# Lead and first block as one list of steps, kept by five queues

## The chip, the cores and the metric

One core of a Trainium2 chip runs the program. A core has a matrix engine (PE), a vector engine (DVE), an activation engine (ACT), a general one (POOL) and SP, which here only issues transfers (the load queue). Every engine works its own queue in order and waits on semaphores for the others. The metric is the device time of one execution in microseconds (us); less is better.

## What is computed

Three layers in a row, all in float32; the first is attention with a complex decay:

```python
mag = np.sqrt(a_re * a_re + a_im * a_im)
scale = np.minimum(mag, 0.999) / (mag + 1e-06)      # a_re, a_im times scale
for t in range(S):                                   # B, H, S, D = 4, 8, 768, 48
    S_re, S_im = ar*S_re - ai*S_im + outer(k, v), ar*S_im + ai*S_re
    y[:, :, t] = einsum(q, S_re)
x = y as 3072 rows of 384
h = x @ w_in;  g = h * tanh(softplus(h));  x = g @ w_out      # d_ff 2048
out = ((x @ w_a) * (x @ w_b)) @ w_out2                         # d_ff 1536
```

## The kernel before, in words

The 768 steps are cut into 6 chunks of 128 for each of 4 batches, so there are 24 chunks c = 0 to 23; block j is the four chunks 4j to 4j+3, 512 rows of x. In a chunk the decay is squared (`decay_1`, step `sq`), added (`add`), taken through Ln and Exp on ACT (`ln`, `ex`), made into an angle (`tan`, `at`) and a size (`ell`); running sums over the chunk are matmuls (`pl`, `pt`); q and k are scaled (`sc`) and rotated (`rq`, `rk`), transposed on PE and copied out by ACT (`tq`, `tk`, `cq`, `ck`), multiplied (`s`), masked on DVE (`cp`), multiplied with v (`py`), and the result is split into a high and a low half for PE (`xh` on ACT, `xl` on DVE). `outer` and `state` (`ou`, `sd`, `st`) bring the state forward.

The second layer is 16 units f for each block. A unit is nine matmuls (`moe1_h`, called h below), a minimum on DVE (mn), four activations (ma, mb), a product on DVE (pr) and the matmuls of `moe1_x2` (x). A block of the third layer has 12 units of 18 and 12 matmuls. The weights of the second layer come as 64-bit numbers: a transfer of 768 KB each (w), then three DVE operations (`decode`: da, dc, db), a rounded copy on ACT (hi, so) and a subtraction on POOL (lo, sl). There are two buffers `wraw` for raw weights, so a third transfer waits until the first is decoded. In block 0 the weights of `w_out` are used as decoded; they are split for block 1 and later.

Before the change only the lead (chunks 0 to 3, three decodes) follows a list written out by hand, kept on DVE, ACT, PE and POOL by `in_order`; the load queue isn't in it. In the lead `load_a` loads the decay of a chunk in two transfers of 192 KB, real and imaginary part; both go by SP, except that the imaginary part of chunk 0 is issued on ACT's queue. `load_a(0)` also loads ACT's Ln/Exp table. From block 0 on the program states the steps unit by unit: chunk steps come at slots (`plan`, `run_to`), weights by `pipeline`, one call of `do_w` a unit. A scheduler of the framework then orders each queue by that sequence and a model of costs, and may take steps out of turn. `behind` keeps the first units after the lead.

ps_h has two buffers, so the h of unit n+2 waits until pr of unit n has read its sum.

Of the kernel before, what the change touches and what calls it, by code (L numbers as in the profile page):

```python
# [21 lines left out]
def kernel(  # L22
# [118 lines left out]

    def load_weights(nm, j, src, pool, place, late=False):

        a, b = src.shape[1:]
        if src.dtype == F32:
            raw = pool.tile([P, a, b], F32, tag="wraw", name="wraw", bufs=2)
            nc.sync.dma_start(out=raw, in_=src)
        else:  # L150
            b //= 2
            raw = pool.tile([P, a, b, 2], U32, tag="wraw", name="wraw", bufs=2)
            nc.sync.dma_start(out=raw.rearrange("p a b t -> p a (b t)"), in_=src)
        f = [raw]

        def decode(first=True, rest=True):
            if late and first:
                f[0] = wps[0].tile([P, a, b], F32, tag="f", name=f"w{nm}{j}", bufs=NF // 2 + 1)
                whole[nm, j] = f[0], split
                if src.dtype == F32:  # L160
                    nc.vector.tensor_copy(f[0], raw)
                    return
            if src.dtype != F32:
                if not late and first:
                    f[0] = pool.tile([P, a, b], F32, tag="wf32", name="wf32")
                fu, low, high = f[0].bitcast(U32), raw[..., 0], raw[..., 1]
                if first:
                    nc.vector.tensor_scalar(fu, high, 3, 0x3FFFFFFF, ALU.logical_shift_left, ALU.bitwise_and)
                    nc.vector.scalar_tensor_tensor(fu, high, 0xC0000000, fu, ALU.bitwise_and, ALU.bitwise_or)  # L169
                if rest:  # L170
                    nc.vector.scalar_tensor_tensor(fu, low, 29, fu, ALU.logical_shift_right, ALU.bitwise_or)

        def split():
            hi = place(f"w{nm}h{j}", [P, a, b])
            if late:
                lo = wps[0].tile([P, a, b], F32R, tag="f", name=f"w{nm}l{j}", bufs=NF // 2 + 1)
            else:
                lo = place(f"w{nm}l{j}", [P, a, b])
            weights[nm, j] = [hi, lo]
            act(out=hi, in_=f[0], func=AF.Copy)  # L180
            nc.gpsimd.tensor_tensor(lo, f[0], hi.bitcast(F32), ALU.subtract)

        return [decode, lambda: None] if late else [decode, split]
# [77 lines left out]
    def in_rows(c, nm):  # L261
# [4 lines left out]
        if nm == "qh":  # L266
            nc.gpsimd.memset(own[:, :, D:], 0.0)
# [77 lines left out]
    def decay_exp(c):  # L345
# [100 lines left out]

    def values(c):
# [4 lines left out]
        if not j:  # L452
# [28 lines left out]
    def store_y2(c):  # L481
        j, b = chunk(c)
        if not j:
            return
        py, yh, yl = st.pop(("y", c))
        nc.vector.tensor_tensor(yl, py, yh.bitcast(F32), ALU.subtract)
        for y, d in zip((yh, yl), yt_d[j]):
            for par in range(2):
# [3 lines left out]
                )  # L492

# [29 lines left out]
    def read_x(c):  # L523
# [4 lines left out]
        if not j:  # L528
# [125 lines left out]

    def load_w2(early):


        for j in range(NF2 // 2):
            def place(name, shape, j=j):
                if j == EARLY:  # L660
                    return wps[0].tile(shape, F32R, tag="f", name=name, bufs=NF // 2 + 1)
# [129 lines left out]
    def pipeline(steps, ahead, loaded=(), decoded=()):  # L791

        loaded, decoded = list(loaded), list(decoded)
# [13 lines left out]
    weights1 = None  # L807

    def do_w():
        next(weights1, None)  # L810

# [20 lines left out]
    def lead_in():  # L832

        for c in range(B):
            load_a(c)
        decode, split = steps1[0]()
        for c in range(B):
            load_qk(c)
        for c in range(B):
            load_v(c)  # L840
        decode_2, split_2 = steps1[1]()
        run_to(slot[0] + 1)
        w_in_1 = steps1[2]()

        def size(c):
            decay_4(c)
            split_ell(c)
# [312 lines left out]
```

## Time and profile before

| | us |
|---|---|
| three timed runs | 1089.99, 1091.11, 1091.15 |
| median | 1091.11 |
| the profiled execution, its own time | 1091.89 |
| its span, first to last instruction | 1090.2 |
| PE busy | 1049.1 (96%) |
| DVE busy | 655.7 (60%) |
| ACT busy | 610.5 (56%) |
| POOL busy | 231.4 (21%) |

The profile is of one execution. All times inside it count from the first instruction. A matmul's end is modelled and consecutive matmuls overlap, so the distance from start to start tells what one costs; the same holds in a smaller measure for DVE and ACT.

### The profile page before, as it was taken

To read this page: it belongs to the slowest core of one execution; us is meant where nothing else is said; L and a number is where in the kernel's file an instruction comes from. 1 tells how busy PE (TensorE), PEld (TensorE's weight loads), DVE (VectorE), ACT (ScalarE), POOL (GpSimd) and SP (SyncE) were. 2 spreads that over 40 slices of the span, in tenths; PEclk is the share of its full clock that TensorE was granted. 3 is DMA by queue.
4 is the path that set the end of the run, shared out by engine and by line. 5 is a ranking of instruction groups with operands and counts; after the bars stand their busy time and mean duration, and the time that the engine had idled before them with its cause. 6 is when DMAs were issued, how large, how long until landed. Compare 5 with 4: busy or idle time off the path is not lost.

```text
span 1090.2 us, 15919 instructions
## 1 busy us (share of the span) xinstructions
PE 1049.1 (96%) x6060; PEld 874.8 (80%) x6060; DVE 655.7 (60%) x998; ACT 610.5 (56%) x968; POOL 231.4 (21%) x265
## 2 busy tenths in 40 slices
PE   4979999999999999999999999999999999999997
PEld 1956666788888888888877778888888888888886
DVE  6898976787777777777589998532322322422222
ACT  7868887898788887788767842221221222212211
POOL 2122333444334334333331123100000000000000
PEclk9999999999999999999999999999999999999999
DMA  9656652354444343343155366110100100100000
GB/s 199 140 155 170 166 152 66 67 96 86 112 81 81 67 95 79 83 102 79 31 164 182 126 217 211 44 58 1 30 29 1 58 1 1 44 1 1 29 1 32
DMA packets 203549, 90.92 MB, mean 83 GB/s; under 512 B 144781, under 2 KB 187850, under 8 KB 203466
## 3 DMA queue, kind: packets, MB, share of 16 engines
q1 hardware_dynamic: 202410, 89.62, 32.9%
q8 instruction: 50, 0.82, 0.3%
q10 hardware_dynamic: 1056, 0.21, 0.1%
q14 instruction: 33, 0.27, 0.1%
HBM read 72.44 MB, written 17.36 MB: 82 GB/s over the span
## 4 chain that ended last, share of the span: by engine, by line
PE 72%; DVE 12%; ACT 6%; issue 4%; DMA 3%; POOL 2%; SPq 1%; ACTq 0%; DVEq 0%; POOLq 0%
PE x2ps L639 12%; PE ops L719 12%; PE hps L596 12%; PE psa L694 11%; PE psb L694 11%; PE psc L435 3%; PE py L465 3%; ACT m L59 3%; PE pkT L412 2%; PE pqT L412 2%; DVE wf L169 1%; ACT L54 1%; DVE m L602 1%; PE pt L331 1%; PE pu L504 1%
## 5 line engine op out<-in xcount | busy, mean ns | idle before, releaser
L705 DVE TENSOR_TENSOR a_sb<-a_sb,psb 128x512 f32<-128x512 f32 x72 | 49.4, 686 | 224.6 <-PE psb L694 224.6
L59 ACT ACTIVATE m<-m 128x512 f32<-128x512 f32 x192 | 119.4, 632 | 62.5 <-DVE m L602 57.7
L59 ACT ACTIVATE a_sb<-psa 128x512 f32<-128x512 f32 x72 | 42.9, 596 | 162.8 <-PE psa L694 160.7
L59 ACT ACTIVATE ph<-a_sb 128x512 fp32r<-128x512 f32 x72 | 45.4, 631 | 156.7 <-DVE a_sb L705 156.7
L596 PE MATMUL hps<-xh,winh 128*128 128x512 f32 x288 | 118.9, 414 | 7.8 <-DVE gh L613 6.4
L623 POOL TENSOR_TENSOR gl<-m,gh 128x512 fp32r<-128x512 f32 x64 | 83.2, 1300 | 151.7 <-DVE gh L622 128.4
L596 PE MATMUL hps<-xl,winh 128*128 128x512 f32 x288 | 114.0, 396 | 0.0
L596 PE MATMUL hps<-xh,winl 128*128 128x512 f32 x288 | 113.9, 396 | 0.0
L719 PE MATMUL ops<-woh,ph 128*128 128x384 f32 x288 | 97.1, 337 | 0.0
L719 PE MATMUL ops<-woh,pl 128*128 128x384 f32 x288 | 97.1, 337 | 0.0
L719 PE MATMUL ops<-wol,ph 128*128 128x384 f32 x288 | 96.7, 336 | 0.0
L639 PE MATMUL x2ps<-gl,wouth 128*128 128x512 f32 x240 | 94.3, 393 | 2.2 <-DVE gl L623 1.2
L639 PE MATMUL x2ps<-gh,wouth 128*128 128x512 f32 x240 | 94.1, 405 | 1.8 <-ACT gh L59 1.5
L639 PE MATMUL x2ps<-gh,woutl 128*128 128x512 f32 x240 | 94.0, 392 | 0.0
L616 DVE SCALAR_TENSOR_TENSOR m<-m,hps 128x512 f32<-128x512 f32 x80 | 54.7, 684 | 62.3 <-ACT m L59 61.5
L694 PE MATMUL psa<-xh,wal 128*128 128x512 f32 x216 | 85.2, 394 | 0.0
L694 PE MATMUL psa<-xl,wah 128*128 128x512 f32 x216 | 85.1, 394 | 0.0
L694 PE MATMUL psa<-xh,wah 128*128 128x512 f32 x216 | 84.4, 391 | 0.6 <-DVE a_sb L705 0.6
L694 PE MATMUL psb<-xh,wbh 128*128 128x512 f32 x216 | 84.2, 390 | 0.0
L694 PE MATMUL psb<-xh,wbl 128*128 128x512 f32 x216 | 84.2, 390 | 0.0
L694 PE MATMUL psb<-xl,wbh 128*128 128x512 f32 x216 | 84.2, 390 | 0.0
L707 DVE TENSOR_TENSOR pl<-a_sb,ph 128x512 fp32r<-128x512 f32 x72 | 52.0, 722 | 39.0 <-ACT ph L59 39.0
(167 smaller groups left out, 2335.8 us busy)
## 6 DMA issues: line engine op xcount, KB each, us to landing
wraw<-in_moe_w_out_dram SPq DMA_DIRECT2D x14, 768.0 KB
wraw<-in_moe_w_in_dram SPq DMA_DIRECT2D x8, 768.0 KB
a<-in_a_re_dram SPq DMA_DIRECT2D x24, 192.0 KB
q<-in_q_dram SPq DMA_DIRECT2D x24, 192.0 KB
k<-in_k_dram SPq DMA_DIRECT2D x24, 192.0 KB
v<-in_v_dram SPq DMA_DIRECT2D x24, 192.0 KB
wraw<-in_moe_w_a_dram SPq DMA_DIRECT2D x6, 768.0 KB
wraw<-in_moe_w_b_dram SPq DMA_DIRECT2D x6, 768.0 KB
```

The source lines that it names most:

```text
L59: x = nc.scalar.activation(**kw)
L412: nc.tensor.transpose(p[:, i, :], src[:, h].rearrange("p a d -> p (a d)") if c < B else own[:, h], ident)
L435: nc.tensor.matmul(p[:, i, :], lhsT=st["kT", c, hf][:, i, :], rhs=st["qT", c, hf][:, i, :], start=True, stop=True)
L465: nc.tensor.matmul(p[par * 64:(par + 1) * 64, i, :], lhsT=w[:, col:col + 64], rhs=x[:, first + par, :], start=(n == 0), stop=(n == len(ter ...
L596: nc.tensor.matmul(p, lhsT=w[:, kk, :], rhs=x[:, kk, :], start=(i == 0), stop=(i == len(ops) - 1))
L616: nc.vector.scalar_tensor_tensor(m, m, 2.5, p, ALU.subtract, ALU.mult)
L623: (nc.vector if on_act else nc.gpsimd).tensor_tensor(gl, m, gh.bitcast(F32), ALU.subtract)
L639: nc.tensor.matmul(x2ps[m], lhsT=w[:, ms], rhs=x, start=(f == 0 and i == 0), stop=(f == NF - 1 and i == len(terms) - 1),)
L694: nc.tensor.matmul(p, lhsT=w[:, kk, :], rhs=x[:, kk, :], start=(i == 0), stop=(i == len(ops) - 1))
L705: nc.vector.tensor_tensor(a_sb, a_sb, pb, ALU.mult)
L707: nc.vector.tensor_tensor(lo, a_sb, hi.bitcast(F32), ALU.subtract)
L719: nc.tensor.matmul(ops_t[t], lhsT=x[:, tsl], rhs=w, start=(f == 0 and i == 0), stop=(f == NF2 - 1 and i == 2),)
```

## The change

The list now covers the lead, all 16 units of block 0, the first two of block 1, and the chunk steps of c = 0 to 7 and part of 8. Every step is a name (`sq3`, `h.4`: the number is the chunk, the unit or the weight in the order in1, out1, in2, ...; `w.3` is the transfer of the second `w_in` weight). Steps that were one call are cut into their instructions (decode into da, dc, db; split into hi, lo; `carry`, `state`, `two_parts`, `decay_exp`, `store_y2`, the memsets). The same operations are executed, and `in_order` now also takes E.SP. Everything after the list is put behind the last instruction of the list on each queue. The tiles of the late `w_out` weights get a fixed place each (`kept`) instead of a ring. Core of the diff:

```diff
+    def kept(n, dt, name):
+        return wps[0].tile([P, 2, DM], dt, tag=f"f{n}", name=name, bufs=1)
...
-        def decode(first=True, rest=True):
+        def decode(part=None):
...
-    def lead_in():
-        for c in range(B):
-            load_a(c)
-        decode, split = steps1[0]()
-        for c in range(B):
-            load_qk(c)
-        for c in range(B):
-            load_v(c)
-        decode_2, split_2 = steps1[1]()
...
-            sq0 add0 ln0 sq1 add1 ex0 ln1 sq2 tan0 ex1 sq3 ell0 add2 pl0 ln2 ex2 ep0 ell1 tan1 at1 add3 pl1 d1
-            at0 tan2 pt1 ln3 ell2 pt0 pl2 sc0 ep1 ex3 red1 red0 sc1 at2 ell3 sin0 tan3 sin1 at3 rq0 rk0 rq1
...
-            px3 xh2 xh3 xl2 xl3 tan4
-    last, after_lead = in_order(first, (E.DVE, E.Activation, E.PE, E.Pool)), traced()
-    do_w()
-    for c in range(B):
-        read_end(c)
+    run("""
+            a1 sq1 add1 ln1 a0 sq0 add0 ex1 tan1 w.1 da.1 ell1 pl1 dc.1 w.2 da.2 db.1 ln0 ex0 dc.2 tan0 at1
+            hi.1 lo.1 ell0 pt1 red1 a3 sq3 add3 at0 pt0 red0 db.2 ep1 a2 sq2 add2 w.3 da.3 ln3 he1 ex3 pl0 ep0
+            ell3 pl3 ln2 he0 ex2 qk0 sc0 sin0 dc.3 tan2 at2 pt2 db.3 hi.3 lo.3 qk1 v3 sc1 sin1 ep3 rq0 tq00
+            cq00 tq10 cq10 ell2 pl2 ep2 red2 rk0 tk10 ck10 s10 rk1 tan3 at3 he2 tk11 ck11 a4 sq4 w.4 v0 w.5
+            da.4 da.5 rq1 tq11 cq11 dc.5 tk00 he3 ck00 tk01 ck01 tq01 cq01 pt3 qk2 sc2 sin2 cp10 dc.4 db.5
+            hi.5 add4 ln4 ht0 ex4 db.4 s00 cp00 s11 cp11 s01 cp01 red3 re0 gm4 lo.5 v2 qk4 v1 qk3 sc3 sin3 py0
+            yt0 py1 ou0 yt1 rk2 tk02 tk12 ck12 rq2 tq02 cq02 tq12 cq12 rq3 tq03 cq03 ck02 px1 w.6 da.6 re2 vm4
+            v4 w.7 rk3 tan4 ell4 st0 cy4 tq13 cq13 s12 tk03 ck03 cp12 da.7 tk13 ck13 at4 s02 cp02 dc.7 re1 a5
+            sq5 add5 xh1 ca4 px0 xh0 ht2 xl0 xl1 s03 cp03 pl4 ep4 em4 he4 re4 s13 cp13 db.7 py2 pt4 red4 ht4
+            ln5 sc4 yt2 ex5 hi.7 ht1 py3 yt3 px2 xh2 xl2 dc.6 px3 xh3 xl3 ou3 ou1 tan5 ell5 db.6 h.0 pl5 h.1
+            sin4 ht3 close mn.0 re3 st3 cy5 vm5 v5 at5 ca5 pt5 rk4 ms4 rq4 ma.0 mb.0 pr.0 w.8 w.9 st1 mn.1
+            red5 tk14 ou2 st2 open so.0 lo.7 ep5 em5 he5 h.2 mn.2 ma.1 mb.1 tq14 ck14 cq14 a6 tq04 cq04 da.8
+            dc.8 so.1 so.2 ma.2 sq6 sl.0 gm5 pr.1 x.0 x.1 sl.1 da.9 dc.9 db.8 db.9 hi.9 lo.9 tk04 ck04 mb.2
+            add6 ln6 h.3 mn.3 ma.3 pr.2 s04 cp04 ht5 re5 qk5 w.10 da.10 w.11 sc5 s14 cp14 ou4 ex6 tan6 ell6
+            ms5 dc.10 h.4 mb.3 pr.3 da.11 db.10 mn.4 at6 sin5 py4 vm6 x.2 x.3 sl.2 pl6 ma.4 mb.4 yt4 dc.11
+            db.11 ep6 rk5 rq5 pr.4 sd4 xl4 st4 hi.11 lo.11 gm6 so.3 h.5 mn.5 ma.5 mb.5 tq15 cq15 w.12 cy6 ca6
+            em6 da.12 h.6 mn.6 x.4 ma.6 so.4 mb.6 tq05 cq05 pr.5 x.5 sl.3 dc.12 w.13 da.13 db.12 dc.13 db.13
...
+            pr.14 mb.15 pr.15 h.16 h.17 mn.16 mn.17 ma.16 mb.16 pr.16 st6 x.14 ma.17 mb.17 pr.17 x.15 st7
+    """)
+    last, after_lead = in_order(first, (E.DVE, E.Activation, E.PE, E.Pool, E.SP)), traced()
+    slot[0] = 50
...
-    for ui in range(len(units) + lag):
-        if ui == 3:
-            behind(after_lead, last)
+    base, want = ends[18 // NF], ends[1 + 18 // NF]
+    for ui in range(18, len(units) + lag):
...
-            do_w()
...
-            if blk == 1 and f % 2 == 0:
+            if blk == 1 and f % 2 == 0 and f // 2 >= 7:
                 whole["out", f // 2][1]()
...
+    behind(after_lead, last)
     allp.close()
```

## Rows read from the trace of the kernel before

**Rows 1.** Page, part 2: busy tenths in 40 slices of 27.25 us.

```profile
PE   4979999999999999999999999999999999999997
DVE  6898976787777777777589998532322322422222
```

**Rows 2.** Windows, core 0: length, then busy us of each engine (count), clock, DMA.

```profile
5.90:52.78 46.88, 36.32 (x242) 29.02 (x242) 38.98 (x68) 40.31 (x66) 3.46 (x17) 1.00 0.91 167
52.78:110.00 57.22, 51.25 (x339) 35.29 (x338) 53.41 (x82) 44.16 (x68) 13.27 (x12) 0.94 0.62 168
110.00:180.00 70.00, 67.40 (x433) 46.20 (x431) 53.63 (x71) 52.83 (x80) 24.47 (x22) 1.00 0.54 136
180.00:220.00 40.00, 36.50 (x227) 29.02 (x226) 30.01 (x48) 35.82 (x56) 17.45 (x21) 1.00 0.30 67
```

**Rows 3.** Timeline, PE: start us, duration us, what; bracket: idle before, and its releaser.

```profile
52.78 0.73 PE L596 MATMUL hps<-xh,winh 128*128 128x512 f32 x2
...
144.36 0.50 PE L596 MATMUL hps<-xh,winh 128*128 128x512 f32 x1
...
148.71 0.79 PE L596 MATMUL hps<-xh,winh 128*128 128x512 f32 x1
...
177.80 2.74 PE L639 MATMUL x2ps<-gh,wout 128*128 128x512 f32 x6
179.97 0.79 PE L596 MATMUL hps<-xh,winh 128*128 128x512 f32 x1
...
186.66 0.50 PE L596 MATMUL hps<-xh,winh 128*128 128x512 f32 x1 [1.42 <-DVE m L616]
```

**Rows 4.** Timeline and chain of waits, first 14 us: transfers and the first angle.

```profile
0.81 0.48 ACTq L220 DMA_DIRECT2D a<-in_a_im_dram  x1
1.32 1.28 ACT L228 ACT_TABLE_LOAD   x1 [1.32 <-PEq L1144]
5.03 0.84 ACT L59 ACTIVATE qhp<-a 128x768 f32<-128x768 f32 x1 [2.42 <-DMA a<-in_a_im_dram]
7.68 5.90 DMA wraw<-in_moe_w_in_dram
8.83 0.56 DVE L291 TENSOR_TENSOR a<-a,r 128x384 f32<-128x384 f32 x1 [0.17 <-ACT r L59]
```

**Rows 5.** Timeline, DVE: three operations without a gap in block 0.

```profile
66.27 0.95 DVE L169 SCALAR_TENSOR_TENSOR wout<-wraw,wout 128x768 uint32<-128x768 uint32 x1
67.13 0.55 DVE L385 TENSOR_TENSOR q<-q,size 128x384 f32<-128x384 f32 x1
67.60 0.95 DVE L171 SCALAR_TENSOR_TENSOR wout<-wraw,wout 128x768 uint32<-128x768 uint32 x1
```

**Rows 6.** Waits of DVE, 8 to 53 us: in total, times, longest.

```profile
DVE s L276 <- ACT s L59: 1.6, 1, 1.6
DVE xl L544 <- ACT xh L59: 1.5, 3, 0.9
...
DVE s L297 <- ACT r L59: 0.2, 1, 0.2
```

**Rows 7.** Timeline, a POOL operation and DVE beside it; then groups by form, 0 to 180 us.

```profile
53.36 1.95 POOL L181 TENSOR_TENSOR winl<-wf,winh 128x768 fp32r<-128x768 f32 x1 [8.80 <-ACT winh L59]
53.52 2.05 DVE L297 TENSOR_SCALAR qhp<-qhp 128x384 f32<-128x384 f32 x1
...
L297 DVE TENSOR_SCALAR qhp<-qhp 128x384 f32<-128x384 f32 x6 | 5.7, 954 | 0.0
L297 DVE TENSOR_SCALAR s<-s 128x384 f32<-128x384 f32 x3 | 1.1, 356 | 0.2 <-ACT r L59 0.2
L181 POOL TENSOR_TENSOR winl<-wf,winh 128x768 fp32r<-128x768 f32 x8 | 16.5, 2062 | 78.2 <-ACT winh L59 78.2
L181 POOL TENSOR_TENSOR woutl<-wout,wouth 128x768 fp32r<-128x768 f32 x8 | 15.9, 1987 | 11.4 <-PE x2ps L639 7.1 <-ACT wouth L59 4.0
```

**Rows 8.** Groups by form on ACT, 0 to 180 us: count, busy, mean ns, idle before.

```profile
L54 ACT ACT_TABLE_LOAD x17 | 21.8, 1283 | 1.2 <-DVE a L356 0.7 <-ACT size L59 0.2
L59 ACT ACTIVATE wouth<-wout 128x768 fp32r<-128x768 f32 x8 | 6.4, 831 | 0.0
```

More of the change, by code (lines that the diff above doesn't have):

```diff
@@ L154, in load_weights @@
         f = [raw]
-        def decode(first=True, rest=True):
-            if late and first:
-                f[0] = wps[0].tile([P, a, b], F32, tag="f", name=f"w{nm}{j}", bufs=NF // 2 + 1)
+        def decode(part=None):
+            if late and part in (None, 0):
+                f[0] = kept(j, F32, f"w{nm}{j}")
                 whole[nm, j] = f[0], split
-                if src.dtype == F32:
+            if src.dtype == F32:
+                if late and part in (None, 0):
                     nc.vector.tensor_copy(f[0], raw)
[L162 to L181, printed above, removed]
+                return
+            if not late and part in (None, 0):
+                f[0] = pool.tile([P, a, b], F32, tag="wf32", name="wf32")
@@ L789, with pipeline @@
         wq += [("in", j, wcols(w_in, j)), ("out", j, wrow(w_out, j))]
-    def pipeline(steps, ahead, loaded=(), decoded=()):
-        loaded, decoded = list(loaded), list(decoded)
+    def pipeline(steps, ahead, loaded=()):
+        loaded, decoded = list(loaded), []
         steps = list(steps)
@@ L830, in behind, with run @@
                 tc.add_manual_dep(x, last[x.engine], no_sync, reason="after the lead")
[L832 to L847 removed]
+    units = [(b, f) for b in range(NB) for f in range(NF)]
+    ready, lag = {}, 2
+    hs, ms, loads = {}, {}, {}
+    late_pools = {}
+    def run(names):
         def turned(c):
@@ new lines, in run, with end_lead, end_first @@
+        for name in names.split():
+            kind, dot, n = name.partition(".")
+            if name in late_pools:
+                late_pools[name]()
+            elif dot:
+                parts[kind](int(n))
+            else:
+                steps[name[:-1]](int(name[-1]))
+    def end_lead():
+        nonlocal mp
+        lead.close()
+        mp = allp.enter_context(tc.tile_pool(name="mp", bufs=3))
+    def end_first():
+        nonlocal ps_x
+        tail.close()
+        ps_x = w1.enter_context(tc.tile_pool(name="ps_x", bufs=1, space=PSUM))
+        wps.append(allp.enter_context(tc.tile_pool(name="wp1", bufs=NF)))
@@ L934 @@
                 next(prep, None)
[L935 to L942 removed]
+        if ui - lag >= 16:
             moe1_x2(*units[ui - lag], *ready.pop(ui - lag))
```

229 lines of the change are left out of this document (143 added, 86 removed).

## The prediction

> **What bounds the kernel now.** I read the slices of the page first: PE is at nine tenths or more from the fourth slice on, up to the last, and DVE at six to nine tenths until 500 us [rows 1]. So past the first stretch only PE counts, and this change leaves that part alone; what it can move lies before the point where its list ends. That point is the end of the matmuls x of unit 15, when the h of unit 18 starts: 179.97 us [rows 3]. The windows split these 180 us [rows 2]. In the lead, up to the first h at 52.78 us [rows 3], PE is idle 10.6 of 46.9 us and DVE works 39.0. From there to 110 us DVE is the fullest engine (53.4 of 57.2 us) and PE loses 6 us and clock: 0.94 granted, a mix of 2.4 and 1.2 GHz. From 110 to 180 PE is busy 67.4 of 70. All later blocks should keep their 910 us, so the question is whether the end of the list moves from 180.
>
> **Costs of a step.** I count a step by the distance from start to start in an unbroken run. On DVE [rows 5] a two-input operation on 384 columns costs 0.47 us, one on 768 columns 0.87; by the same reading of the timeline a masked copy or a minimum costs 0.6, a one-input operation on 384 0.28, the angle's reduction 1.5 and a whole decode 2.2 to 2.5, taken as 2.39. On PE a pair of h and x takes 148.71 - 144.36 = 4.35 us [rows 3], other pairs up to 4.65; I take h 2.07 and x 2.6. The attention of a chunk takes four groups of transposes at 0.44, scores 1.78, values 1.9, state 0.92 and two sums at 0.65.
>
> **DVE ahead of the first h.** DVE works its queue in the order of the list, so everything named before `xl3` lies on the path to h.0. Before, that was four chunks at 7.6 us (add, tan 0.47 each, size 0.75, scaling 0.94, reduction 1.5, two rotations 1.74, two masks 1.24, xl 0.5), three decodes (7.2) and 0.5 for chunk 4: 38.1 us. In the new list it is the same four chunks (30.4), six whole decodes (w.1 to w.5 and w.7: 14.3) and two thirds of w.6 (1.5), chunk 4 up to its scaling (4.6), add5 and st0 (0.9): 51.7 us. So 13.6 us of block 0's DVE work moves ahead of h.0. It leaves block 0 with less to do, but the lead gets longer.
>
> **The start.** The list begins with chunk 1, and `a0` stands behind `ln1`. The imaginary half of chunk 0 goes by ACT's queue, which the list keeps too: what was issued at 0.81 us [rows 4] now waits behind sq1, a table load and ln1. Chunk 1 should be there at about 5.2 (chunk 0 was at 5.03 [rows 4]); sq1 costs 0.75, the table load, no longer hidden in the wait for data, 1.28; so ln1 and then the transfer are issued near 7.4. It lands 4.2 us after its issue at the least (0.81 to 5.03) and 5.9 at the most (a weight behind other transfers) [rows 4]: 11.6 to 13.3, taken as 12.0, nearer to the row of the same transfer. On ACT sq0 and ex1 follow, and tan1, which stands ahead of the first decode on DVE, runs at 13.6. Before, the first tan ran at 8.83 [rows 4]. The weight da.1 needs will have landed, but can't be used earlier.
> The Trainium skill, "DMA: Bandwidth & Descriptors", section "Queues, rings and completion order", says that each DMA engine takes turns between the queues that have work. ACT's transfer would then share with w.2 and chunk 3 on SP's queue and take about twice its own time, 1 us more by an estimate from 192 KB at the lead's rate; no row here shows two loaded queues, and the sum goes without it.
>
> **The first h.** From tan1 on, 51.7 - 0.9 (add1, add0) = 50.8 us of DVE work stand up to xl3: 13.6 + 50.8 = 64.4. Two things come on top. First, subtractions on POOL (lo.1, lo.3, lo.5) fall into a stretch in which DVE is full. The trace shows what that does: beside a POOL operation of 53.36 to 55.31 a DVE operation of 0.36 us took 2.05, ending with it [rows 7]. Before, lo.1 cost DVE 0.3, lo.3 1.7 and the third 1.2; I take 1.2 for each, 3.6, between 0 and three whole ones (5.9). Second, waits: before, the eight kinds in the lead sum to 7.4 us, the first 1.6 of it at the start [rows 6], so 5.8; with decodes to fill gaps I take 2.5, between 0 and 5.8. This includes SP: w.3 waits for db.1 (two raw buffers), and qk0, qk1 and v3 are queued behind it on SP; w.3 is issued near 18.4, so q and k of chunk 0 land by 26, about when DVE has worked its way to sc0. h.0 then starts at 70.5 (64.0 to 77.4), 17.7 later than now.
>
> **Block 0.** From h.0 to the end of x.15 the list has for PE 18 h (37.3), 16 x (41.6), the transposes, scores, values and states of chunks 4 to 7 (25.4), seven sums (4.6) and ou2 (0.9): 109.8 us. Now the same stretch holds 113.6 and takes 127.2, so 13.6 are lost. In the new list PE is clearly the fullest engine behind h.0: DVE has 76.8 us left and ACT 92. Weights are decoded a pair of units ahead. By count, pr.4, which h.6 waits for (two buffers), has 26.3 us of DVE work ahead of it since h.0, and h.6 has 32.5 on PE; the other units stand no worse. I take 3 us lost, between 0 and 13.6. End of the list: 70.5 + 109.8 + 3 = 183.3, against 180.0: 3.3 later.
>
> **What costs nothing.** The split of `w_out` moves from block 1 into the list in the text only: its eight copies on ACT already ran before 180 us [rows 8]. The list changes ACT's table 19 times and load_a(0) adds one, against 17 and one [rows 8]: 2.6 us more on ACT, which has some 40 us of slack over the list. Fixed tiles for `w_out`, memsets as steps of their own: POOL is idle three quarters of this time [rows 2], so its cover holds. Everything behind the list now waits for its last step on each queue; SP's last are q, k of chunk 8 and y, x of chunks 6 and 7, needed half a block later. In exchange the arctangent of chunk 8 is in the list; now its two table loads delay a product and PE idles 1.42 us at 186.66 [rows 3]. I take back 0.7 (0 to 1.4).
>
> **Sum.** +3.3 - 0.7 = +2.6 us. On the profiled execution (1091.89, 0.8 above the median of 1091.11) that is 1094.5, on the median 1093.7. All bounds at their low end give 64.0 + 109.8 - 1.4 = 172.4, 7.6 less; at their high end 200.8, 21 more.
>
> **Rivals.**
> *The list runs as it stands*: POOL costs DVE nothing, the decodes fill all waits, PE loses 1 us in block 0: 64.4 + 109.8 + 1 - 0.7 = 174.5, 5.5 earlier, 1085.6. For it: DVE's prefix has no step that must wait long, and PE loses hardly more from 110 on even now [rows 2]. Against it: rows 7.
> *POOL holds DVE in block 0 as well.* Five POOL subtractions (lo.7, sl.0, sl.1, lo.9, sl.2) stand between h.0 and pr.4. DVE is 32.5 - 26.3 = 6.2 us ahead there, so from 1.24 us an operation on, pr.4 is late for h.6, PE stops and loses clock, as it did between 53 and 110. If block 0 then loses at its present rate (13.6 of 127.2, so 11.7 here), the list ends at 192.0: +11.3, 1102.4. For it: the single event of rows 7; against it: summed over all forms, DVE was stretched by 14 us beside 20 POOL operations, 0.7 each.
> The Trainium skill, "SBUF — State Buffer", section "SBUF: two separate sides", gives the rule: POOL and DVE share one pair of ports, whoever starts first holds it for the whole instruction, and a DVE operation with two inputs from SBUF fully waits. By it each subtraction would cost up to its 2 us, which speaks for this rival; the event of rows 7 agrees, the mean of 0.7 shows how often DVE reads PSUM or is idle at that time.
> *The start isn't delayed*: the transfer on ACT's queue comes as early as now, which the list's text hides. Then DVE begins 4.8 us earlier and, with 0.8 of that lost in new waits, the sum is -1.4: 1089.7.
>
> **Chances.** About 0.2% (2.2 us) is what a measurement can tell from no change here. My forecast 0.47, of which 0.27 is slower and 0.20 within 0.2%; its own range is 1090 to 1098. The list as it stands 0.27, faster. POOL in block 0 0.15, slower. No delayed start 0.11, of which 0.08 is within and 0.03 faster. Together faster 0.30, same 0.28, slower 0.42. The range reaches from the first rival to the second: 1085 to 1102.
>
> **What would show it.** In the new profile: the first tan near 13.6 us and the imaginary half of chunk 0 issued on ACT's queue near 7.4; the first h near 70 with DVE over nine tenths before it; DVE operations of 2 us beside POOL's; PE busy without gaps from h.0 and the full clock; h of unit 18 near 183. It is wrong if the first h comes before 65, if PE in block 0 still loses over 6 us, or if the stretch after the list changes by more than 2 us.

## The result: slower by 0.65%, and the profile after

The changed kernel takes 1097.9 us (median of 4, 1096.7 to 1099.8) against 1090.8 (median of 4): ratio 1.0065, 95% interval 1.0051 to 1.0080. The forecast was 1093.7 with a range of 1085 to 1102. The sign is as forecast, the size 4.2 us short. Profiled against profiled it is 1097.46 against 1091.89, spans 1095.7 and 1090.2: 5.5 us to be found in the trace, 5.2 of them by the end of the list. Line numbers have moved: h is L647 (was L596), x L703 (L639), the minimum L653, the product `pr` L677 (L613), a decode's three steps L172, L174, L176, the subtractions on POOL L188 (L181), the first angle L303 (L291).

The page's slices first (part 2; 40 slices of 27.4 us, busy tenths):

```profile
PE   2799999999999999999999999999999999999997
DVE  4998865877777776767679998632322322422222
```

PE and DVE are emptier in the first two slices than in [rows 1]; in the third PE is fuller (9, was 7), and from the fourth on its digits are as they were. The windows (length, then busy us and count of PE, PEld, DVE, ACT, POOL; clock, DMA share, GB/s) answer to [rows 2]:

```profile
5.90:70.00 64.10, 42.90 (x312) 32.82 (x314) 54.07 (x90) 53.73 (x81) 8.33 (x19) 0.87 0.77 158
70.00:110.00 40.00, 37.73 (x241) 26.07 (x237) 34.46 (x51) 32.29 (x50) 12.95 (x13) 0.96 0.56 157
110.00:186.00 76.00, 76.00 (x467) 52.15 (x466) 51.66 (x82) 61.73 (x92) 16.11 (x15) 1.00 0.44 103
186.00:226.00 40.00, 36.84 (x230) 29.61 (x229) 31.68 (x50) 33.52 (x53) 20.53 (x26) 1.00 0.56 142
```

The lead is 64 us long instead of 47, with 54.1 us of DVE work in it instead of 39.0. Behind it PE loses 2.3 us up to 110 and nothing at all from there to the end of the list; before it lost 6.0 and 2.6.

The timeline of after shows where it was lost (start, duration, engine, line, what; in brackets the idle time before and its releaser). First the start:

```profile
5.01 1.28 ACT L59 ACT_TABLE_LOAD   x1 [5.01 <-DMA a<-in_a_im_dram]
6.30 0.84 ACT L59 ACTIVATE s<-a 128x768 f32<-128x768 f32 x1
7.17 1.28 ACT L54 ACT_TABLE_LOAD   x1
7.78 0.43 ACTq L228 DMA_DIRECT2D a<-in_a_im_dram  x1
8.46 0.84 ACT L59 ACTIVATE s<-s 128x768 f32<-128x768 f32 x1
9.32 1.28 ACT L236 ACT_TABLE_LOAD   x1
13.96 0.84 ACT L59 ACTIVATE qhp<-a 128x768 f32<-128x768 f32 x1 [3.35 <-DMA a<-in_a_im_dram]
...
15.56 0.56 DVE L303 TENSOR_TENSOR a<-a,r 128x384 f32<-128x384 f32 x1 [0.18 <-DMA a<-in_a_im_dram]
...
70.35 0.50 PE L647 MATMUL hps<-xh,winh 128*128 128x512 f32 x1
```

The imaginary half of chunk 0 is issued at 7.78, lands 6.2 us later, and there are three table loads ahead of sq0, one more than the prediction had: with the preload of `load_a(0)` moved back, one stands before the first square as well. The first angle runs at 15.56, not at 8.83 [rows 4]. Yet the first h starts at 70.35. Then block 0, DVE and POOL beside PE:

```profile
80.16 1.82 POOL L188 TENSOR_TENSOR winl<-wf,winh 128x768 fp32r<-128x768 f32 x1 [8.22 <-DVE W L566]
80.55 1.88 DVE L172 TENSOR_SCALAR wout<-wraw 128x768 uint32<-128x768 uint32 x1
81.93 2.17 POOL L188 TENSOR_TENSOR woutl<-wout,wouth 128x768 fp32r<-128x768 f32 x1
82.46 2.46 DVE L174 SCALAR_TENSOR_TENSOR wout<-wraw,wout 128x768 uint32<-128x768 uint32 x1
84.84 0.67 DVE L677 SCALAR_TENSOR_TENSOR gh<-m,hps 128x512 f32<-128x512 f32 x1
...
85.57 4.29 PE L703 MATMUL x2ps<-gh,wout 128*128 128x512 f32 x6 [2.27 <-DVE gh L677]
...
180.43 5.31 PE L703 MATMUL x2ps<-gh,wout 128*128 128x512 f32 x12
185.18 0.79 PE L647 MATMUL hps<-xh,winh 128*128 128x512 f32 x1
```

Two decode steps of 0.55 and 0.95 us (da.8, dc.8) take 1.88 and 2.46 beside POOL's lo.7 and sl.0. The product pr.1 stands behind them, x.1 waits 2.27 us for it, and its six matmuls then take 4.29 us instead of 2.74. The last group is x.14 and x.15; h of unit 18 follows 4.75 us later in this kernel and in every one below.

### The profile page after: what moved, and what is told of

The parts are those of the page before. It is cut to its first block, busy times and chain, and to the rows that moved or that the text cites. A ratio compares the mean times of both kernels' runs of the same rounds, so it can differ in the third digit from the quotient of the medians.

```text
span 1095.7 us, 15885 instructions
## 1 busy us (share of the span) xinstructions
PE 1049.9 (96%) x6060; PEld 875.2 (80%) x6060; DVE 651.3 (59%) x998; ACT 616.4 (56%) x970; POOL 230.5 (21%) x265
## 4 chain that ended last, share of the span: by engine, by line
PE 76%; ACT 7%; DVE 7%; issue 5%; DMA 2%; POOL 2%; SPq 1%; ACTq 0%; DVEq 0%; POOLq 0%
PE ops L787 14%; PE psa L762 13%; PE psb L762 13%; PE x2ps L703 13%; PE hps L647 11%; PE py L505 3%; ACT m L59 3%; PE psc L472 3%; PE pkT L449 1%; PE pu L549 1%; ACT L54 1%; PE pqT L449 1%; DMA a<-in_a_im_dram 1%; SPq L228 1%; PE pt L352 1%
## 5 line engine op out<-in xcount | busy, mean ns | idle before, releaser
L647 PE MATMUL hps<-xh,winh 128*128 128x512 f32 x288 | 117.2, 408 | 0.9 <-DVE m L680 0.9
L647 PE MATMUL hps<-xh,winl 128*128 128x512 f32 x288 | 112.9, 392 | 0.0
L647 PE MATMUL hps<-xl,winh 128*128 128x512 f32 x288 | 112.7, 391 | 0.0
L703 PE MATMUL x2ps<-gl,wouth 128*128 128x512 f32 x240 | 94.7, 395 | 2.2 <-DVE gl L687 1.2
L703 PE MATMUL x2ps<-gh,wouth 128*128 128x512 f32 x240 | 93.8, 404 | 1.8 <-ACT gh L59 1.5
L703 PE MATMUL x2ps<-gh,woutl 128*128 128x512 f32 x240 | 94.0, 392 | 0.0
L680 DVE SCALAR_TENSOR_TENSOR m<-m,hps 128x512 f32<-128x512 f32 x80 | 54.6, 683 | 63.3 <-ACT m L59 62.7
L653 DVE TENSOR_SCALAR m<-hps 128x512 f32<-128x512 f32 x96 | 65.5, 683 | 21.1 <-PE hps L647 20.8
```

Source lines behind the costliest of these rows:

```text
L647: nc.tensor.matmul(p, lhsT=w[:, kk, :], rhs=x[:, kk, :], start=(i == 0), stop=(i == len(ops) - 1))
L680: nc.vector.scalar_tensor_tensor(m, m, 2.5, p, ALU.subtract, ALU.mult)
L703: nc.tensor.matmul(x2ps[m], lhsT=w[:, ms], rhs=x, start=(f == 0 and i == 0), stop=(f == NF - 1 and i == len(terms) - 1),)
```

## The experiments

My theory after the result: the late start costs about 6 us up to the end of the list, and the stall of x.1 with the slower clock behind it about 4. The rival for the start: it is absorbed by waits in the lead. The rival for the stall: DVE is simply full there, and any gain comes back as another wait.

The table has all kernels by the same three moments, with the time from the first h to x.14, and PE's waits in it. In three kernels whose clock stayed full after h.0 (e4, e6, e9), that time less the waits is 106.1 us each (108.37 - 2.27 = 106.10 for e4). What is over this elsewhere is put down to the clock, as an inference: the column is that remainder and not a reading. In after it fits, since the granted clock was 0.68 from 85 to 90 us; in e12_raw_early the clock was full, and the 0.3 is not explained. The ratio is to the kernel before, measured beside each.

Behind the list, where all kernels have the same steps, the profiled executions took 908.7 to 911.2 us from the h of unit 18 to the end. So a difference of 1 to 2 us between two medians need not come from the edit, and the moments inside the list tell more.

| kernel | first angle | h.0 | x.14 | h.0 to x.14 | PE waits | clock | median us | ratio, 95% |
|---|---|---|---|---|---|---|---|---|
| after | 15.56 | 70.35 | 180.43 | 110.08 | 2.3 | 1.7 | 1097.9 | 1.0065 (1.0051 to 1.0080) |
| e1_a0_early | 9.82 | 64.44 | 174.51 | 110.07 | 2.3 | 1.7 | 1090.6 | 0.9995 (0.9986 to 1.0005) |
| e2_pool_later | 16.32 | 73.10 | 183.12 | 110.02 | 2.2 | 1.7 | 1099.8 | 1.0071 (1.0058 to 1.0084) |
| e3_both | 9.89 | 66.38 | 176.41 | 110.03 | 2.2 | 1.7 | 1090.4 | 0.9989 (0.9978 to 1.0000) |
| e4_free_loads | 16.05 | 71.02 | 179.39 | 108.37 | 2.3 | 0 | 1095.4 | 1.0038 (1.0023 to 1.0052) |
| e5_decode_later | 10.01 | 67.04 | 182.60 | 115.56 | 6.3 | 3.2 | 1098.7 | 1.0061 (1.0047 to 1.0075) |
| e6_pr1_first | 9.95 | 64.73 | 173.62 | 108.89 | 2.8 | 0 | 1090.8 | 0.9990 (0.9981 to 0.9999) |
| e7_copies_later | 16.17 | 70.26 | 181.36 | 111.10 | 3.4 | 1.6 | 1097.0 | 1.0049 (1.0034 to 1.0064) |
| e8_a0_by_sp | 12.26 | 69.18 | 179.22 | 110.04 | 2.3 | 1.7 | 1095.1 | 1.0031 (1.0020 to 1.0041) |
| e9_adds_on_dve | 16.18 | 71.19 | 179.62 | 108.43 | 2.3 | 0 | 1095.9 | 1.0041 (1.0026 to 1.0057) |
| e10_clear | 10.16 | 65.08 | 178.34 | 113.26 | 4.9 | 2.3 | 1094.2 | 1.0030 (1.0016 to 1.0045) |
| e11_clear_free | 9.96 | 67.01 | 179.60 | 112.59 | 4.9 | 1.6 | 1094.7 | 1.0030 (1.0019 to 1.0040) |
| e12_raw_early | 9.82 | 66.41 | 175.25 | 108.84 | 2.4 | 0.3 | 1089.7 | 0.9987 (0.9978 to 0.9996) |

### The start: e1_a0_early and e8_a0_by_sp

```diff
-            a1 sq1 add1 ln1 a0 sq0 add0 ex1 tan1 w.1
+            a1 a0 sq1 add1 ln1 sq0 add0 ex1 tan1 w.1
```

> The only edit to the changed kernel: step a0 moves ahead of sq1, so the imaginary half of chunk 0 is issued on ACT's queue at the start and the Ln/Exp table is loaded once. Theory (the delayed start sets the first h, since DVE is full from the first tan on): first tan at 9 us in place of 15.6, first h at 64 to 65 in place of 70.4, end of the list and span 5.5 us earlier (4.5 to 6.5), timed 1092.4, ratio to the kernel before 1.0015. Rival (the transfers of the lead, now asked for earlier, or another wait take the place of the delay): first tan at 9 us too, but first h not before 68, ratio 1.005 or more.

One step moved three places in the list. It is as the theory had it: the first angle comes 5.74 us earlier, the first h 5.91, x.14 5.92. The median falls by 7.3 us, back to the time before; the 1.3 us beyond these moments lie behind the list in the two profiled executions. ACT's timeline of e1_a0_early shows both halves of the gain: the transfer issued at once, and one table load hidden under it.

```profile
0.81 0.49 ACTq L228 DMA_DIRECT2D a<-in_a_im_dram  x1
1.33 1.28 ACT L236 ACT_TABLE_LOAD   x1 [1.33 <-PEq L1230]
6.00 0.84 ACT L59 ACTIVATE s<-a 128x768 f32<-128x768 f32 x1 [3.38 <-DMA a<-in_a_im_dram]
...
8.22 0.83 ACT L59 ACTIVATE qhp<-a 128x768 f32<-128x768 f32 x1
```

The other one leaves the order and the table loads and only takes the transfer off ACT's queue:

```diff
-        load_one(c, a_im, t[:, 1], nc.sync if c else nc.scalar)
+        load_one(c, a_im, t[:, 1], nc.sync)
```

> The kernel after, with the imaginary half of chunk 0 of a issued by SP instead of by ScalarE's queue; the order of steps and the table loads of ScalarE are unchanged. It separates the two halves of the late start: the transfer that lands late and the two table loads around ln1. Theory (the transfer holds sq0 until about 14 us, and the table loads alone would let it run at 10.6): first tan at 12.0 to 12.6, h.0 at 66.5 to 67.5, median 1094 to 1095. Rival (the table loads are all of it, or the transfer by SP is as late): first tan at 15 or later, and the median at 1096.5 to 1099.

ACT's timeline of e8_a0_by_sp:

```profile
5.05 1.28 ACT L59 ACT_TABLE_LOAD   x1 [5.05 <-DMA a<-in_a_im_dram]
...
7.21 1.28 ACT L54 ACT_TABLE_LOAD   x1
...
9.36 1.28 ACT L236 ACT_TABLE_LOAD   x1
10.65 0.84 ACT L59 ACTIVATE qhp<-a 128x768 f32<-128x768 f32 x1
```

sq0 runs straight behind the third table load, and the first angle at 12.26: of the 5.74 us, 3.30 are the transfer and 2.44 the table loads and the order around them. The median is about as the theory had it (1095.1), but the first h is only 1.2 us earlier than after, not 3.4. In this execution DVE waited 3.0 us for the score matmuls instead of 0.9. PE starts the long group of scores at 44.53 us, 2.7 earlier than after (47.22), and loses 1.5 of that on the way to the first h: the lead has a second bound, which comes next.

### The second bound of the lead: e5_decode_later, and e1 against e3

```diff
-            ... px1 w.6 da.6 re2 ... cp12 da.7 tk13 ... cp02 dc.7 re1 ... cp13 db.7 py2 ... ex5 hi.7 ht1 ... xl2 dc.6 px3 ... ell5 db.6 h.0 ...
+            ... px1 w.6 re2 ... cp12 tk13 ... cp02 re1 ... cp13 py2 ... ex5 ht1 ... xl2 px3 ... ell5 h.0 ...
...
-            ... gm5 pr.1 x.0 x.1 sl.1 da.9 dc.9 db.8 db.9 hi.9 lo.9
+            ... gm5 pr.1 da.7 dc.7 db.7 hi.7 lo.7 w.8 da.6 sl.0 x.0 x.1 sl.1 dc.6 db.6 w.9
...
-            ... pr.2 s04
+            ... pr.2 da.8 dc.8 da.9 dc.9 db.8 db.9 hi.9 lo.9 s04
```

> The list of e1_a0_early, with more of the decoding of the later weight chunks behind the first PSUM product of unit 1 (pr.1): chunk 6's and 7's remaining steps (da.6, dc.6, db.6, da.7, dc.7, db.7, hi.7) and so 3.9 us of DVE work leave the stretch before h.0, and chunk 8's da and dc go behind pr.2. Theory (the lead up to h.0 is set by DVE, and the stall of 2.2 us at x.1 with the slower clock behind it by decode steps that stand ahead of pr.1): h.0 at 60 to 61 instead of 64.4, no wait at x.1, median 1082 to 1084, that is 7 to 8 us below e1_a0_early. Rival (block 0 is so full on DVE that what is taken out ahead of it comes back as waits of PE behind pr.1): h.0 early, but x.14 and x.15 end within 2 us of e1_a0_early's 174.5, and the median stays at 1089 to 1092.

The theory fell, and by more than its rival had. With 3.9 us of DVE work taken out, the first h came 2.6 us later than in e1_a0_early. DVE's waits in the lead and PE's in block 0 (us in total, times, longest):

```profile
DVE am L478 <- PE psc L472: 4.0, 3, 1.7
...
PE py L505 <- DVE am L478: 6.3, 2, 3.7
```

And the windows up to 60 us, first of e1_a0_early (from 30), then of e5_decode_later and of e3_both (from 40); the lead of e3_both has the same list as that of e1_a0_early:

```profile
30.00:40.00 10.00, 8.11 (x32) 6.00 (x31) 9.93 (x16) 6.81 (x13) 0.82 (x5) 1.00 1.00 191
40.00:50.00 10.00, 10.00 (x110) 9.63 (x109) 9.25 (x15) 9.49 (x16) 2.32 (x11) 1.00 0.52 137
50.00:60.00 10.00, 10.00 (x86) 9.47 (x84) 9.57 (x18) 9.59 (x18) 0.00 (x0) 1.00 0.42 85
```

```profile
40.00:50.00 10.00, 10.00 (x93) 9.61 (x91) 8.37 (x14) 9.33 (x15) 2.21 (x10) 0.93 0.49 118
50.00:60.00 10.00, 10.00 (x88) 9.58 (x86) 7.05 (x14) 7.59 (x14) 0.11 (x1) 0.90 0.50 110
```

```profile
40.00:50.00 10.00, 10.00 (x98) 9.50 (x97) 8.88 (x14) 9.11 (x14) 2.21 (x10) 0.84 0.57 143
50.00:60.00 10.00, 10.00 (x84) 9.67 (x82) 8.16 (x16) 7.88 (x15) 0.11 (x1) 0.94 0.43 87
```

DVE sets the lead up to 40 us (9.9 of 10). From 40 us on PE has no idle time left in any of the three. From the long group of scores (24 matmuls) to the first h PE's timeline has one wait, of 0.23 us, and the distance is 23.13 us in after, e1, e4, e6, e7 and e10 and 24.65 to 24.70 in e2, e3, e5, e8, e11 and e12 (25.74 in e9, which has one wait of 0.79 more). So PE sets this stretch in every kernel here, whenever it begins. The two lengths go with the pace of PE's matmuls; the first `ou` in e1_a0_early, e5_decode_later and e11_clear_free:

```profile
47.59 1.14 PE L549 MATMUL pu<-v,kh 128*64 128x48 f32 x32
48.67 1.95 PE L549 MATMUL pu<-v,kh 128*64 128x48 f32 x32
48.63 1.95 PE L550 MATMUL pu<-v,kh 128*64 128x48 f32 x32
```

e11_clear_free, a kernel of a later section, has the 3.9 us of DVE work in its lead that e5_decode_later lacks. Both have a granted clock of 0.93 and 0.90 from 40 to 60 us, and their first h starts at 67.01 and 67.04: the decodes taken out there only freed DVE for a wait, and e5's lead is longer than e1's for PE's pace. What counts is PE's clock: in e5_decode_later it was 0.93 and 0.90, and in e3_both 0.84 and 0.94, where the same list as e1_a0_early reached the first h 1.9 us later (66.38 against 64.44; DVE's wait for scores 2.5 against 0.8 us). That the clock differs between executions of one list in the lead is shown by these two; why it does, no run settles.

### The stall of x.1: e2, e3, e9 and e7

```diff
-            red5 tk14 ou2 st2 open so.0 lo.7 ep5 ... sq6 sl.0 gm5 pr.1 x.0 x.1
+            red5 tk14 ou2 st2 open so.0 ep5 ... sq6 gm5 pr.1 lo.7 sl.0 x.0 x.1
```

> The only edit to the changed kernel: the POOL subtractions lo.7 and sl.0 move behind pr.1; the order of DVE is untouched. Theory (POOL holds DVE's da.8 and dc.8, so pr.1 is late and PE stops for 2.3 us and then runs x.1 at half clock): da.8 and dc.8 take 0.55 and 0.95 us in place of 1.88 and 2.46, no wait of x.1, 0.83 granted clock gone from that stretch, span 4.4 us earlier (3.5 to 4.5), timed 1093.5, ratio 1.0025. Rival (da.8 and dc.8 are long for another reason, or the next product is late then): less than 1 us gained, ratio 1.0055 to 1.0065.

> Both edits: a0 ahead of sq1, and lo.7 and sl.0 behind pr.1. Theory (two delays one after the other, both on the path): gains add, 9.9 us, timed 1088.0, ratio 0.9975, faster than both kernels. Rival (with the start earlier, DVE or ACT is the bound in block 0 and one gain hides the other): 5 to 6 us, ratio 1.001.

(e3_both has the edit of e1_a0_early too.) These two tell nothing of the cause: a step's place in the list binds an engine only against that engine's other steps. POOL has nothing else to do there, so lo.7 still ran when its data were there, in e2_pool_later at 82.91, beside da.8 at 83.29 with 1.85 us. The stall stayed at 2.2 us. e3_both is e1_a0_early again, and its time is the same.

The next kernel takes the two subtractions off POOL and leaves DVE's queue up to pr.1 as it was (its list is that of e2_pool_later):

```diff
-                nc.gpsimd.tensor_tensor(lo, f[0], weights[nm, j][0].bitcast(F32), ALU.subtract)
+                eng = nc.vector if (nm, j) in (("in", 3), ("out", 0)) else nc.gpsimd
+                eng.tensor_tensor(lo, f[0], weights[nm, j][0].bitcast(F32), ALU.subtract)
```

> The kernel after, with the two subtractions lo.7 and sl.0 done by DVE behind pr.1 instead of by GpSimd ahead of it; all other steps in their order. GpSimd then has no tensor operation between the lead and x.1, without any change to DVE's work ahead of pr.1. Theory (GpSimd's subtractions stretch DVE's two decode steps): da.8 at 0.55 us and dc.8 at 0.95 us instead of 1.9 and 2.5, no wait at x.1, and since DVE now carries 1.9 us more behind pr.1 the next wait, of the score matmuls for ScalarE's kT copy that queues behind hi.9, stays at 0 to 1.5 us: 1094 to 1096. Rival (these decode steps are long for another reason, such as the transfers then running): da.8 and dc.8 stay at 1.9 and 2.5 us, x.1 waits longer than 2 us, 1098 to 1100.

DVE in e9_adds_on_dve (line numbers from 188 on are one higher), and PE's next wait:

```profile
81.37 0.55 DVE L172 TENSOR_SCALAR wout<-wraw 128x768 uint32<-128x768 uint32 x1
81.96 0.96 DVE L174 SCALAR_TENSOR_TENSOR wout<-wraw,wout 128x768 uint32<-128x768 uint32 x1
...
83.43 0.95 DVE L189 TENSOR_TENSOR winl<-wf,winh 128x768 fp32r<-128x768 f32 x1
...
91.52 2.05 PE L473 MATMUL psc<-qT,kT 128*128 128x128 f32 x16 [2.31 <-ACT kT L59]
```

This settles the cause: without POOL beside them the same two steps take 0.55 and 0.96 us, and x.1 doesn't wait. Nor was it the transfers, the rival's cause: from 80 to 85 us they moved 154 GB/s here and 41 in after. On DVE the subtraction costs 0.95 us, on POOL it costs DVE 1.3 to 1.5 (1.88 - 0.55, 2.46 - 0.96). But a wait of 2.31 us now stands at the scores, where up to 1.5 was expected, and the gain over after is 2.0 us, not 4: about as much as the clock, which stayed full.

```diff
-            ... ln5 sc4 yt2 ex5 hi.7 ht1 ... open so.0 lo.7 ep5 em5 he5 h.2 mn.2 ma.1 mb.1 tq14
+            ... ln5 sc4 yt2 ex5 ht1 ... open ep5 em5 he5 h.2 mn.2 ma.1 mb.1 hi.7 so.0 lo.7 tq14
```

> The kernel after, with ScalarE's copies hi.7 and so.0 behind mb.1, so that GpSimd's lo.7 and sl.0, which need them, run later; DVE's order is as it was. It asks whether GpSimd's additions stretch da.8 and dc.8. Theory (they do): da.8 and dc.8 take 0.5 and 0.9 us instead of 1.9 and 2.5, and no wait stands at x.1 if GpSimd's additions then fall clear of pr.1; 1093 to 1095. Rival (they are long by themselves at this place, or GpSimd's additions only meet the next DVE steps): x.1 still waits 2 us, and the time stays at 1097 to 1100.

Here the subtractions come later because ACT's copies do. DVE and PE in e7_copies_later:

```profile
80.45 0.55 DVE L172 TENSOR_SCALAR wout<-wraw 128x768 uint32<-128x768 uint32 x1
81.03 0.96 DVE L174 SCALAR_TENSOR_TENSOR wout<-wraw,wout 128x768 uint32<-128x768 uint32 x1
...
83.70 2.21 DVE L172 TENSOR_SCALAR wf<-wraw 128x768 uint32<-128x768 uint32 x1 [1.12 <-POOL winl L188]
...
91.70 2.79 PE L472 MATMUL psc<-qT,kT 128*128 128x128 f32 x16 [3.43 <-ACT kT L59]
```

da.8 and dc.8 are short again, POOL now holds da.9 (2.21 us), and the scores wait 3.43 us. The theory was right on the cause, the rival on the time.

### Block 0 is a chain of waits: e6, e10, e11, e12

```diff
-            ... a6 tq04 cq04 da.8
-            dc.8 so.1 so.2 ma.2 sq6 sl.0 gm5 pr.1 x.0 x.1
+            ... a6 tq04 cq04
+            so.1 so.2 ma.2 sq6 sl.0 gm5 pr.1 da.8 dc.8 x.0 x.1
```

> The list of e1_a0_early, with chunk 8's da and dc behind pr.1 on DVE and nothing else moved. Theory (the two long decode steps, beside GpSimd's lo.7 and sl.0, are what x.1 waits for, and the half clock behind that wait costs about as much again): no wait at x.1, its six matmuls at 2.3 to 2.7 us instead of 4.3, median 1086 to 1088, 3 to 4 us below e1_a0_early. Rival (the wait is only moved, to the next step that DVE owes PE): the median stays at 1089.5 to 1091.5, and another group of PE shows the wait.

The rival's case. x.1 doesn't wait any more, and the scores do. ACT in e6_pr1_first shows for what:

```profile
84.17 0.84 ACT L59 ACTIVATE winh<-wf 128x768 fp32r<-128x768 f32 x1 [3.90 <-DVE wf L176]
84.92 0.58 ACT L59 ACTIVATE kT<-pkT 128x512 f32<-128x512 f32 x1
```

The copy of kT could have run earlier (in the next kernel it does, at 81.08), but hi.9 stands ahead of it on ACT's queue and waits 3.90 us for DVE's db.9. So e10_clear, with lo.7 on DVE and a0 as in e1_a0_early, moves db.8, db.9 and hi.9 too:

```diff
-            ... open so.0 lo.7 ep5 ... tq04 cq04 da.8
-            dc.8 so.1 so.2 ma.2 sq6 sl.0 gm5 pr.1 x.0 x.1 sl.1 da.9 dc.9 db.8 db.9 hi.9 lo.9 tk04 ck04 mb.2
-            add6 ln6 h.3 mn.3 ma.3 pr.2 s04 cp04 ht5 re5 qk5 w.10 da.10 ...
+            ... open so.0 ep5 ... tq04 cq04
+            so.1 so.2 ma.2 sq6 gm5 pr.1 lo.7 da.8 dc.8 x.0 x.1 da.9 dc.9 tk04 ck04 mb.2
+            add6 ln6 h.3 mn.3 ma.3 pr.2 db.8 db.9 hi.9 lo.9 s04 cp04 ht5 re5 qk5 sl.0 sl.1 w.10 da.10 ...
```

> The list of e1_a0_early with block 0 cleared of both waits seen so far: lo.7 on DVE behind pr.1, chunk 8's da and dc behind it, chunk 9's db and hi behind pr.2, so that ScalarE's kT copy of ck04 no longer queues behind hi.9, and sl.0, sl.1 behind the memsets of qk5 on GpSimd. Theory (block 0 has waits for want of order, not of engine time, since DVE is busy 2/3 of the stretch from 110 us): PE without a gap from h.0 at 64.4 to x.15, no half clock, x.14 and x.15 at 170 to 171 against e1_a0_early's 174.5; median 1086 to 1088. Rival (another step that DVE or ScalarE owes PE comes late in its place, as in e6_pr1_first): a new wait of 2 us or more between 75 and 110 us, median 1090 to 1092.

> e10_clear with the load queue left to its own order (SP out of the ordered engines). Theory (with the lead set by DVE and block 0 by PE, the order of loads binds nothing): within 1 us of e10_clear. Rival (free loads are worth here what they were over the kernel after): 2 us or more below e10_clear.

The stretch from h.0 to 89 us has no gap, and then PE stands for 4.90 us. It is the rival's case, and dearer than it had: 1094.2 us against 1090 to 1092. SP, DVE and PE in e10_clear:

```profile
85.33 0.37 SPq L157 DMA_DIRECT2D wraw<-in_moe_w_out_dram  x1
...
90.45 0.71 DVE L172 TENSOR_SCALAR wout<-wraw 128x768 uint32<-128x768 uint32 x1 [3.62 <-DMA wraw<-in_moe_w_out_dram]
...
94.39 0.70 PE L506 MATMUL py<-am,v 128*64 128x128 f32 x4 [4.90 <-DVE am L479]
```

A later db.8 gives its raw buffer back later (there are two), so w.10 is issued at 85.33 and lands 5.1 us on; da.10 waits 3.62 us for it on DVE, ahead of cp14, the second mask of chunk 4. A product between the two (91.08 us) then takes 2.15 us instead of 0.55, beside POOL's sl.0 and sl.1 (from 88.94, 3.88 us). e11_clear_free shows the same wait of 4.9 us: free loads don't help, since the buffer holds the load, not the order on SP. (e4_free_loads, below, is 2.5 us better than after with its wait unchanged.) The last kernel takes this cause away: db.8 and db.9 back in front, da.10 behind the masks, POOL's subtractions later still.

```diff
-            ... pr.1 lo.7 da.8 dc.8 x.0 x.1 da.9 dc.9 tk04 ck04 mb.2
-            ... pr.2 db.8 db.9 hi.9 lo.9 s04 cp04 ht5 re5 qk5 sl.0 sl.1 w.10 da.10 w.11 sc5 s14 cp14 ou4
+            ... pr.1 lo.7 da.8 dc.8 x.0 x.1 da.9 dc.9 db.8 db.9 tk04 ck04 mb.2
+            ... pr.2 hi.9 s04 cp04 ht5 re5 qk5 w.10 w.11 sc5 s14 cp14 da.10 lo.9 ou4
```

> e10_clear with the two causes of its wait taken away: chunk 8's and 9's db stand ahead of the product of unit 2 on DVE, so that the raw buffers come free 4 us earlier and w.10 is issued earlier, and da.10, which stood ahead of the second masked copy of cp14 while it waited for that load, stands behind it. lo.9 is on DVE too, and GpSimd's sl.0 to sl.4 are each two places later, clear of the stretch before 95 us. Theory (e10_clear's block 0 lost 4.9 us to da.10's wait for its load plus about 2.5 us of half clock behind it, and nothing else waits): no wait of PE over 0.5 us between h.0 and x.15, x.14 and x.15 at 170.5 to 172 against 178.3, median 1086 to 1088. Rival (block 0 needs DVE and the two raw buffers as early as the list after had them, so that a wait is pushed to the next step each time): another wait of 2 us or more before 115 us, median 1090 or above.

PE's waits from 64 to 186 us in e12_raw_early:

```profile
PE hps L648 <- DVE gh L678: 1.8, 2, 1.4
PE pqT L450 <- DVE W L560: 0.6, 1, 0.6
```

No wait is left between h.0 and 100 us; three small ones (0.6, 0.5 and 1.4) stand behind it, where DVE, with two subtractions more and POOL's beside it, is now busy 14.9 of 15 us (95 to 110). Its median is the lowest, 1089.7 us: ratio 0.9987 (0.9978 to 0.9996) to the kernel before, some 8 us below the one after; the intervals of e1, e3 and e6 overlap with its own. Neither forecast holds as it stands: no wait of 2 us came, and the theory's 1086 to 1088 was not reached; its first h, 66.41 against the 64.44 that I had reckoned with, and the 2.4 us of waits make up the rest. Against the kernel before, 0.13% is less than what I had called tellable.

### The load queue: e4_free_loads

```diff
-    last, after_lead = in_order(first, (E.DVE, E.Activation, E.PE, E.Pool, E.SP)), traced()
+    last, after_lead = in_order(first, (E.DVE, E.Activation, E.PE, E.Pool)), traced()
```

> The only edit to the changed kernel: the load queue is left out of the kept order, so that the scheduler places the transfers on SP; the four other queues keep the list. Theory (SP's order is not on the path, the delayed transfer is on ACT's queue): same time as the changed kernel within 1.5 us, 1096.4 to 1099.4, first h at 70 to 71. Rival (head of line waits on SP, such as the third weight ahead of q and k, hold the lead): 3 us or more gained, first h before 68.

The window of 85 to 90 us, after and then e4_free_loads:

```profile
85.00:90.00 5.00, 4.43 (x8) 1.93 (x9) 4.15 (x6) 1.73 (x3) 0.00 (x0) 0.68 0.70 122
```

```profile
85.00:90.00 5.00, 3.77 (x13) 2.20 (x14) 4.96 (x7) 2.10 (x4) 0.75 (x1) 1.00 0.22 15
```

The lead is no shorter (71.02), and the wait of x.1 is the same 2.3 us. What differs in the profile is the clock behind that wait: 1.00 instead of 0.68, 1.7 us by the table, of the 2.5 in the medians. The time, 1095.4, lies between the theory's span and the rival's. Whether the order on SP has to do with the clock, or the clock is that of this one execution, isn't settled; over e10_clear, free loads gained nothing.

## Why the prediction was right on the sign, and 4.2 us short

**The start.** Mechanism right, size short by 2.0 us. The issue was put at 7.4 and came at 7.78. The landing was put at 12.0 within 11.6 to 13.3 and came at 13.96, 6.2 us after the issue, more than either row had shown. In before the same transfer took 4.2 us, and SP's queue was loaded there too, from 0.81 us on, with transfers of 192 KB; so that no row shows two loaded queues, as the prediction says, was not so. In after two weights of 768 KB (issued at 2.84 and 3.59) were on SP's queue. The prediction named what could add to the time: the Trainium skill ("DMA: Bandwidth & Descriptors", section "Queues, rings and completion order") has loaded queues take turns, an estimate of 1 us more. The 2.0 us beyond the 4.2 have its sign; no run separates turns between queues from the mere load. The third table load was not seen, and it hides behind the transfer in after; in e8_a0_by_sp it is what is left.

**The first h.** Put at 70.5, came at 70.35, by two misses that cancel. From the first angle 54.6 us pass to the end of xl3, against 56.9: DVE's own work was about as counted (50.3 against 50.8), POOL cost 3.1 us in two places (1.97 and 2.05 us for operations of 0.35 and 0.56) against 3.6, and DVE's waits behind the first angle were 1.2 us, against 2.5 taken. That DVE alone sets the lead holds up to 40 us. From the scores at 47.22 us on PE's own chain of 23.13 us sets the first h, which the prediction didn't have. That DVE's count gave the same moment is luck in part: DVE was nearly as full there (9.80 of 10 us from 50 to 60, 9.55 from 60 to 70), and for e5_decode_later, with less work on DVE, the same count gave 60 to 61 and the first h came at 67.04.

**Block 0.** The failed step is "the other units stand no worse". The prediction counted DVE's queue up to pr.4 and h.6 and found 6.2 us in hand; the unit that was late is pr.1, and x.1 behind it, 14 us after the first h. It is the second rival's mechanism, at another place and a third of its price: 2.3 us idle and 1.7 of clock, against 11.7. e9_adds_on_dve shows the cause. The Trainium skill ("SBUF — State Buffer", section "SBUF: two separate sides") states that whoever of POOL and DVE starts first keeps the ports that they share for the whole operation. The trace agrees, with 1.88 for 0.55 and 2.46 for 0.95 us; da.8, the first of the two, has one input from SBUF. The total loss of 4.0 against 3 taken was near; PE's own work was 106.1 + 4.75 = 110.85 us, 1.0 above the 109.8 counted. The list ends at 185.18 against 183.3.

**The tail.** The 0.7 us to be taken back were not there. The wait of 1.42 us at [rows 3] shrank to 0.93, but those for the rotated q and k grew from 2.7 to 4.0 us over the rest, and from the end of the list to the end of the span it is 910.5 us against 910.2, less than the spread of 908.7 to 911.2 that the other kernels show there.

**The sum.** 1.9 us more in the list, 1.0 in the tail, and 1.3 that lies between the medians and the two profiled executions.

**The third rival** is what e1_a0_early made of the kernel: with the start not delayed it forecast 1089.7, measured 1090.6 beside 1091.3 for the kernel before. **The first rival**, the list as it stands with 1085.6, was never reached: e12_raw_early, without most of the waits, came to 1089.7.

So the change does what it is for: PE's loss in block 0 went from 13.6 us to 4.0. The lead, longer by 17.6 us of which some 6 were the late start, ate it up; without the late start the two are even.

## What to carry to other kernels

When a written order is kept by a queue that also issues transfers, read the list once for its transfers alone: one step three places too late cost 5.9 us here up to the end of the list and 7.3 in the medians, as much as the change lost. An order found with the durations of a trace knows nothing of operations that hold each other (POOL beside DVE), of buffers that delay a load, or of the clock; each wait that was cured here brought out the next in line, so look at the time between two moments as work plus waits plus clock, and not at the wait that was there first. And a step's place binds only its own engine.

## What of the hardware was not expected

- POOL's subtraction held DVE steps with one input from SBUF as well (0.35 and 0.55 us became 1.97 and 1.88), while a minimum and a product that read PSUM ran in their usual 0.68 and 0.69 us beside it (e5_decode_later, 85.33 and 85.95, with POOL at work from 84.94 for 4.27 us).
- The same wait of 2.2 to 2.3 us at x.1 was followed by a granted clock of 0.66 to 0.70 over 5 us in five kernels (after, e1, e2, e3, e8) and by the full clock in one (e4_free_loads). The six matmuls of x.1 took 4.29 us in after and 2.84 in e4_free_loads.
- The granted clock that the profile shows and the length of matmuls don't always agree. From 30 to 40 us its row is 1.00 in e1_a0_early and 0.50 in e6_pr1_first (2.4 and 1.2 GHz), but PE was busy 8.11 of 10 us in both, and the same two matmuls (`pl`, at 31.12 and 31.26 us) took 1.65 us in both; in e3_both, with a row of 0.71, they took 0.91. So a row of the clock is to be read beside the lengths. For the first `ou`, between 47 and 57 us, the two go together: it took 1.14 us where the row of its 10 us has 0.94 to 1.00, and 1.91 to 1.95 where it has 0.83 to 0.93.
